# An attention and token-mixing kernel: the scale of u from a bound on u in place of its measured maximum, with the work order searched anew

## The chip, the cores and the metric

The kernel runs on one NeuronCore of one Trainium2 chip. The metric is device time in microseconds (us), the median of several runs of one compiled program. A second number, the span, is the time from the first to the last instruction of one execution that was taken with the hardware profiler on; all rows below are from that execution.

Names of engines: PE multiplies matrices (PEld is its loading of stationary operands), DVE and POOL do elementwise work and reductions, ACT does activations and scaled copies, SP issues most DMA transfers. Each engine runs its instructions in the order in which the program lists them.

## The reference, cut to what matters

Inputs q, k, v have the shape [8 batches, 8 heads, 576 positions, 64]. Each batch goes through the same steps:

```python
out_d = sm_attn(mean4(q), mean4(k), mean4(v))      # attention on means over 4 positions
out_up = np.repeat(out_d, 4, axis=2)
out_local = local_attn(q, k, v)                    # |i - j| < 4
x = (out_up + out_local)                           # -> [8, 576, 512]
xt = x.transpose(0, 2, 1)
h = np.maximum(xt @ w_tok1, 0.0) @ w_tok2          # 576 -> 256 -> 576, along positions
u = x + h.transpose(0, 2, 1)
h2 = np.maximum(u @ w_ch1, 0.0) @ w_ch2            # 512 -> 1536 -> 512, along channels
return u + h2
```

## The kernel before, in words

**Numbers in two halves.** The dense products run in 16-bit floats. Each operand y is scaled by a power of two s, the 16-bit rounding of s*y is kept as its upper part, and the rest as its lower part; `mm3` (line 134) makes three products of the parts (upper-upper, upper-lower, lower-upper). ACT makes the upper parts by a scaled copy, DVE the lower parts by one `scalar_tensor_tensor`. So before u can be split, s must be known on all 128 partitions.

**How s is found for u.** In `mix`, the stream `takes` (line 736) reads u out of PSUM: for each of four channel blocks c and two chunks ch of positions (256 and 320) ACT copies the block to `u` (line 755), and DVE takes the largest absolute value of each row into a column of `umx` (line 757). When all blocks are there, `scale_of` calls `everywhere` (line 669): DVE reduces the columns to one (line 673, tile `um_m`), PE transposes it (line 676, `um_t`), DVE reduces the row (line 679), PE spreads the value to all partitions by a product with ones (line 682, `um_b`), and `pow2` (lines 140 to 142) makes the scale `us` and its inverse `ui`. I call these steps the chain.

**The batches.** Batch 0 takes the plain way: `scaled` finds a scale for each chunk (two chains) and splits u into `uh` (lines 781 and 783), `first` makes the 512 to 1536 product tile by tile (12 tiles of 128 rows, with matmuls written "c<-uh,CW" in the trace), and `second` the 1536 to 512 product. Batches 1 to 7 use seven block products in place of eight (Strassen's scheme in Winograd's form) for the first channel product, and batches 2 to 7 for the second too. For this, `mixtures` forms sums of quarter blocks of u on POOL (line 804, eight instructions of 288 columns a batch: s1, s2, s4, s3), `upper` casts the seven operands on ACT (line 820, 14 instructions a batch), `lower` makes the lower parts on DVE (line 831, 14 a batch), and `product7` multiplies ("P<-a11h,CW" is the first of the seven). One chain a batch serves them all.

**Weights.** The inputs w_ch1 and w_ch2 arrive as 64-bit values and are converted on the chip (`to_f32`: ACT line 241, POOL lines 244 and 247, DVE line 252), then scaled and split (`parts`, lines 374 and 376): tile CW is the first channel weight, CX the second. The sums of weight blocks that the seven products need are written to DRAM once and read back in each batch through SP (tiles `t`, `w_a`, `w_s`, in six buffers of tag `ts`).

**What sets the order.** Every part of the program is a Python generator (a stream) that yields one step at a time: an engine, an estimated duration, what it needs, and which PSUM banks it takes or gives. `drive` (line 182) picks among the streams' next steps the one that could start first by a planner's clocks; among those of one engine that could start within 0.15 us of it, the one whose name stands first in the list `ORDER` (line 36) is taken. The list names about 330 streams (e3.7 is the eighth channel stream of batch 3, n5.2 the third stream of mix of batch 5, b4.6 an attention stream). Until both chunks of batch 0 are split, `drive` also puts filler products (`keep_busy`, line 175) on PE where it would idle. The order that comes out is fixed at compile time, for all engines and for the DMA issues of SP.

**Where the change acts.** `BUFS` (line 72), `value_scale` (line 320, makes `up`, `down` and `big` from the largest sum of squares of v, chain `vm`), `First.scale` (line 389), `everywhere` (669), `takes` (736), `scale_of` (761), `scaled` (769), `upper` (809), and `ORDER` with `SWITCH` (what the planner adds when PE changes the kind of its work).

Of the kernel before, what the change touches and what calls it, by code (L numbers as in the profile page):

```python
# [6 lines left out]
F32 = mybir.dt.float32  # L7
# [7 lines left out]
ALU = mybir.AluOpType  # L15
AX = mybir.AxisListType
# [17 lines left out]
SWITCH = 0.1  # L34
SHARED = 1.4
ORDER = ("e7.9 n3.2 e3.11 b3.3 b3.1 b5.0 n6.2 A6 b4.6 n4.3 e5.6 e6.11 W1 b5.6 n5.3 b3.2 e7.2 b7.9 W0 m4 n7.4 "
# [11 lines left out]
         "e3.7 e3.13 b2.5 b4.4 b4.5 e4.12 e1.7 h2 e3.2 C2 C5 e2.5 n4.5 e2.4 e4.3 C6 n7.5 b6.4 b5.3 ").split()  # L48
# [7 lines left out]
def tile_ups_attention_mixer(ctx, tc, qk, vw, vr, w1, w2, c1, c2, out):  # L56
# [15 lines left out]
    BUFS = dict(cw=6, h=6, vm=2, bs=2, bs2=4, w=4, xh=2, x=5, u=6, uh=7, ts=6, qk=4, qd=1, vw=2, vd=1, pt=2, od=1, sm=10, ev=4, nm=4, qs=1, sc=20)  # L72
# [247 lines left out]
    def value_scale(st):  # L320
# [6 lines left out]
        e = yield step("V", 0.8, give="g")  # L327
        root(big, 2.0 ** 20, st.big[:, 0:1], st.big[:, 1:2])
        nc.vector.tensor_mul(st.up, whole[:, 0:1], st.big[:, 1:2])
        nc.vector.tensor_mul(st.down, whole[:, 1:2], st.big[:, 0:1])  # L330
        make(("scale", b), e)
# [48 lines left out]
    class First(Channel):  # L380
# [8 lines left out]
        def scale(self):  # L389
            for q in range(NQ):  # L390
# [4 lines left out]
                root(big, 2.0 ** (4.5 + 0.5 - 8), self.inv[q], self.s[q])  # L395
# [273 lines left out]
    def everywhere(name, cols, n=128):  # L669

        m = T([n, 1], F32, "ev", f"{name}_m")
        yield step("V", 0.08)
        nc.vector.tensor_reduce(m, cols, axis=AX.X, op=ALU.max)
# [11 lines left out]
    def mix(st):  # L685
# [50 lines left out]
        def takes():  # L736
            for f in range(2):
# [7 lines left out]
                st.hid.append(ht)  # L745
            make(("hid", b), e)
            st.umx = T([128, 2, 4], F32, "sc", f"umx{b}")
            st.u = {}
            for ch, two in WALK[b > 0]:
                s0, N = CHUNKS[ch]  # L750
                for c in (2 * two, 2 * two + 1):
                    yield step("A", 0.06 + N * 0.00113, ("t2", b, ch, c), give=f"gg>{b}" if c % 2 else "")
                    if ch == 0:
                        st.u[c] = T([128, S], F32, "u", f"u{b}_{c}")
                    nc.scalar.activation(st.u[c][:, s0:s0 + N], banks[ch, c // 2][:, c % 2, :N], AF.Copy, scale=st.down)  # L755
                    e = yield step("V", 0.05 + N * 0.00112)
                    nc.vector.tensor_reduce(st.umx[:, ch, c:c + 1], st.u[c][:, s0:s0 + N], axis=AX.X, op=ALU.max,  # L757
                                            apply_absolute_value=True)
                    make(("u", b, ch, c), e)

        def scale_of(ch, cols):
            big = yield from everywhere(f"um{b}_{ch}", cols)
            inv = st.ui[ch] = T([128, 1], F32, "sc", f"ui{b}_{ch}")
            s = T([128, 1], F32, "sc", f"us{b}_{ch}")
            yield step("V", 0.45, give="g")
            pow2(big, 2.0 ** -5, inv, s)
            return s
# [636 lines left out]
```

## Time and profile before

| | us |
|---|---|
| median of 3 runs | 914.3 (912.48 to 918.25) |
| the profiled execution, its own time | 922.99 |
| its span | 921.2 |
| PE busy | 860.3 (93%) |
| DVE busy | 681.7 (74%) |
| ACT busy | 496.0 (54%) |
| POOL busy | 395.1 (43%) |
| granted PE clock, mean over the span | 0.963 of 2.4 GHz |

How to read it: the profiled execution is one run with the profiler on, and its own time, 922.99 us, is its span and 1.8 us around it; it is 8.7 us (1.0%) above the median of the timed runs. A busy PE is not a PE at its peak, since matmuls are pipelined. Idle time of an engine that nobody waits for costs nothing.

### The profile page before, as it was taken

Reading aid. Unit: us, or ns where it says so; the run is one execution under the profiler, and the core shown is the slowest. Engines: PE = TensorE matmul, PEld = TensorE weight load, DVE = VectorE, ACT = ScalarE, POOL = GpSimd, SP = SyncE. Lnnn points to the kernel's source line nnn. Section 1 sums busy time; section 2 is a strip of 40 time slices with the busy share of each in tenths; the row PEclk is TensorE's granted clock in tenths of the full one; section 3 lists DMA queues with packets and bytes.
Section 4 is the critical chain, followed back from the end, with each engine's and each line's share of the span. In section 5 each row is a group of like instructions: output and inputs, shape, how many; then the busy total and the mean of one; then the engine's idle time right before and its main releaser. Section 6 shows DMA issues by size and latency. Waiting matters only on the chain.

```text
span 921.2 us, 27379 instructions
## 1 busy us (share of the span) xinstructions
PE 860.3 (93%) x10961; PEld 640.2 (69%) x10969; DVE 681.7 (74%) x1564; ACT 496.0 (54%) x1208; POOL 395.1 (43%) x585
## 2 busy tenths in 40 slices
PE   6867799999998899989999899999999999999997
PEld 3534587867775777778776677678776767777775
DVE  7677879885877587884797759685899627955962
ACT  4545675435653347672577536764587435734640
POOL 4686784387424783740215521362247120212220
PEclk8756899999999999999999999999999999999999
DMA  8735333172336635725516544734555243245245
GB/s 255 218 126 195 109 133 83 48 239 80 87 85 180 163 108 174 161 64 170 148 54 204 161 120 127 202 115 140 150 167 153 68 123 113 69 140 159 80 130 164
DMA packets 101583, 125.85 MB, mean 137 GB/s; under 512 B 20016, under 2 KB 87344, under 8 KB 100208
## 3 DMA queue, kind: packets, MB, share of 16 engines
q1 hardware_dynamic: 100816, 123.51, 45.9%
q8 instruction: 86, 1.41, 0.7%
q10 hardware_dynamic: 640, 0.59, 0.2%
q14 instruction: 41, 0.34, 0.1%
HBM read 104.40 MB, written 17.30 MB: 132 GB/s over the span
## 4 chain that ended last, share of the span: by engine, by line
PE 59%; DVE 25%; ACT 5%; DMA 4%; issue 4%; POOL 1%; SPq 1%; DVEq 0%; ACTq 0%; POOLq 0%
PE P L136 17%; PE t L136 8%; PE R L136 8%; PE c L136 6%; PE Q L136 4%; PE av L660 3%; PE ad L590 2%; PE t L726 2%; PE busy L180 2%; DVE h L1015 1%; PE pT L647 1%; PE sd L562 1%; PE td L581 1%; PE sc L624 1%; DVE P L636 1%
## 5 line engine op out<-in xcount | busy, mean ns | idle before, releaser
L136 PEld LDWEIGHTS <-CW 128*128 128x128 f16 x1296 | 124.1, 98 | 43.0 <-issue 10.7
L1049 POOL TENSOR_TENSOR g<-r,g 128x288 f16<-128x288 f32 x36 | 29.7, 825 | 169.6 <-ACT g L1038 162.5
L136 PEld LDWEIGHTS <-w_s 128*128 128x128 f16 x864 | 83.1, 98 | 23.2 <-DMA w_s<-sums_s 1.6
L136 PEld LDWEIGHTS <-t 128*128 128x128 f16 x756 | 73.3, 98 | 20.2 <-issue 0.6
L136 PEld LDWEIGHTS <-w_a 128*128 128x128 f16 x648 | 62.5, 99 | 23.7 <-DMA w_a<-sums_a 5.0
L510 POOL TENSOR_TENSOR vr<-vr 72x256 f32<-72x256 f32 x64 | 49.0, 766 | 66.9 <-ACT dump L506 66.5
L136 PE MATMUL c<-h,CX 128*128 128x256 f16 (+1 forms) x576 | 76.6, 287 | 0.0
L136 PEld LDWEIGHTS <-CX 128*128 128x128 f16 x576 | 55.3, 98 | 15.1 <-issue 1.2
L755 ACT ACTIVATE u<-t,down 128x256 f32<-128x256 f32 (+1 forms) x64 | 30.2, 498 | 64.4 <-PE t L136 64.2
L136 PE MATMUL P<-h,w_a 128*128 128x288 f16 x432 | 59.3, 291 | 5.0 <-DMA w_a<-sums_a 3.4
L136 PE MATMUL t<-xh,W 128*128 128x512 f16 (+1 forms) x240 | 59.9, 390 | 2.6 <-DVE xh L704 2.6
L757 DVE TENSOR_REDUCE umx<-u 128x1 f32<-128x256 f32 (+1 forms) x64 | 27.9, 448 | 44.3 <-ACT u L755 44.2
L136 PE MATMUL P<-g,w_s 128*128 128x288 f16 x432 | 58.2, 286 | 0.9 <-DMA w_s<-sums_s 0.9
L536 POOL TENSOR_TENSOR qs<-qk 128x288 f32<-128x288 f32 x56 | 43.9, 785 | 30.1 <-DMA qk<-in_qk_dram 27.2
L136 PE MATMUL t<-W,hid 128*128 128x256 f16 (+1 forms) x384 | 54.8, 291 | 1.0 <-ACT u L755 1.0
L804 POOL TENSOR_TENSOR s<-u,u 128x288 f32<-128x288 f32 x14 | 10.8, 797 | 103.0 <-ACT u L755 103.0
L574 ACT ACTIVATE pd<-sd,nmd 72x144 f32<-72x144 f32 x128 | 37.6, 373 | 28.6 <-DVE nmd L569 26.6
L506 ACT ACTIVATE dump<-vr 72x512 uint8<-72x512 f32 x64 | 40.3, 630 | 18.9 <-DMA vr<-in_vr_dram 18.7
L590 PE MATMUL ad<-vd,ptd 72*72 72x65 f32 x512 | 40.6, 234 | 6.0 <-POOL vd L511 2.0
L704 DVE SCALAR_TENSOR_TENSOR xh<-x,back,xh 128x512 f16<-128x512 f32 (+1 forms) x40 | 33.6, 839 | 15.6 <-ACT xh L702 15.6
L590 PEld LDWEIGHTS ad<-vd,ptd 72*72 72x72 f32 x512 | 38.7, 150 | 9.2 <-POOL vd L511 4.2
L665 ACT ACTIVATE x<-av,up 128x512 f32<-128x512 f32 (+1 forms) x40 | 27.3, 688 | 32.6 <-PE av L660 32.6
(224 smaller groups left out, 2190.5 us busy)
## 6 DMA issues: line engine op xcount, KB each, us to landing
qk<-in_qk_dram SPq DMA_DIRECT2D x32, 579.0 KB
w_s<-sums_s SPq DMA_DIRECT2D x144, 128.0 KB
t<-sums SPq DMA_DIRECT2D x126, 128.0 KB
w_a<-sums_a SPq DMA_DIRECT2D x108, 128.0 KB
vw<-in_vw_dram SPq DMA_DIRECT2D x32, 351.0 KB
vr<-in_vr_dram SPq DMA_DIRECT2D x64, 144.0 KB
C_raw<-in_c_dram SPq DMA_DIRECT2D x16, 512.0 KB
out_dram<-u SPq DMA_DIRECT2D x48, 144.0 KB
```

Source lines behind the costliest of these rows:

```text
L136: nc.tensor.matmul(ps, lhs(a), rhs(c), start=first and i == 0, stop=last and i == 2, **kw)
L506: nc.scalar.activation(dump, t.rearrange("p r c -> p (r c)"), AF.Square, scale=2.0 ** -20, accum_out=st.vm[:, i:i + 1])
L510: nc.gpsimd.tensor_add(t[:, 0:2], t[:, 0:2], t[:, 2:4])
L536: nc.gpsimd.tensor_add(two, x[:, :, 0:2], x[:, :, 2:4])
L574: nc.scalar.activation(pd[:, par, g], s[:, par, g], AF.Exp, bias=nm[:, par, g:g + 1], scale=0.125 / 16)
L590: nc.tensor.matmul(ps[:, g, par], pt[:, par, kg, G * g:G * g + G], st.vd[:, kg, 2 * pr + par], start=kg == 0, stop=kg == 1)
L660: nc.tensor.matmul(ps[QB * j:QB * j + QB, par, D * hp:D * hp + D], pt[p, hp, QB * j:QB * j + QB], st.vw[h][p, g, D * hp:D * hp + D], start ...
L665: nc.scalar.activation(x.rearrange("p hp two d -> p two hp d"), ps[:n, :, :4 * D].rearrange("p two (hp d) -> p two hp d", hp=4), AF.Copy, ...
L704: nc.vector.scalar_tensor_tensor(st.xh[t][:, 1], xf(t), back[:n], st.xh[t][:, 0], ALU.mult, ALU.subtract)
L755: nc.scalar.activation(st.u[c][:, s0:s0 + N], banks[ch, c // 2][:, c % 2, :N], AF.Copy, scale=st.down)
L757: nc.vector.tensor_reduce(st.umx[:, ch, c:c + 1], st.u[c][:, s0:s0 + N], axis=AX.X, op=ALU.max, apply_absolute_value=True)
L1049: e_.tensor_tensor(o[:, 1], plain[p, FROM[x]], o[:, 0], ALU.subtract)
```

## The change

It removes the eight row maxima of u in each batch (64 DVE instructions) and the chain behind them. In their place the largest upper half of `hid` (the hidden values of the token product, known before u) is taken by one DVE reduction over 1024 elements of 16 bits a batch, spread by the same chain, and put into a bound: most = 516 * down * max(hid) + 4 * big, with `down` and `big` from `value_scale`, by one more small DVE instruction. The scale comes from that bound. Batch 0 uses one scale for both chunks (one chain in place of two) and casts each block of u as soon as that block is there. Two small DVE instructions are added in `value_scale`, 8 times. The constants in `pow2` and in `First.scale` change by factors of 4. The buffers of two tags of small tiles change, `SWITCH` goes from 0.1 to 0.05, and the list `ORDER` is another.

```diff
--- before.py
+++ after.py
@@ -31,21 +31,21 @@
 
 SLACK = 0.4
 HOP = 0.2
-SWITCH = 0.1
+SWITCH = 0.05
 SHARED = 1.4
-ORDER = ("e7.9 n3.2 e3.11 b3.3 b3.1 b5.0 n6.2 A6 b4.6 n4.3 e5.6 e6.11 W1 b5.6 n5.3 b3.2 e7.2 b7.9 W0 m4 n7.4 "
 ...
-         "e3.7 e3.13 b2.5 b4.4 b4.5 e4.12 e1.7 h2 e3.2 C2 C5 e2.5 n4.5 e2.4 e4.3 C6 n7.5 b6.4 b5.3 ").split()
+ORDER = ("e3.11 e6.8 e7.13 e1.3 e5.4 e3.9 b3.5 W1 n7.2 e7.8 e5.11 e6.11 b5.7 b3.0 e7.1 U0 a7 e6.1 H0 b2.4 m4 "
 ...
+         "P1 P0 b4.4 e5.13 A1 b7.5 n2.0 M1 e6.5 e6.2 e6.13 e7.0 b7.3 e7.7 e6.7 e1.7 n5.3 b5.6 b5.4 ").split()
 PX = 7
 PATH = [(c, ch) for ch in range(2) for c in range(4)], [(c, ch) for c in range(4) for ch in range(2)]
 WALK = ((0, 0), (0, 1), (1, 0), (1, 1)), ((0, 0), (1, 0), (0, 1), (1, 1))
@@ -69,7 +69,7 @@
     sb = ctx.enter_context(tc.tile_pool(name="sb", bufs=1))
     dram = ctx.enter_context(tc.tile_pool(name="dram", bufs=1, space=bass.MemoryType.DRAM))
     psum = ctx.enter_context(tc.tile_pool(name="psum", bufs=1, space=bass.MemoryType.PSUM))
-    BUFS = dict(cw=6, h=6, vm=2, bs=2, bs2=4, w=4, xh=2, x=5, u=6, uh=7, ts=6, qk=4, qd=1, vw=2, vd=1, pt=2, od=1, sm=10, ev=4, nm=4, qs=1, sc=20)
+    BUFS = dict(cw=6, h=6, vm=2, bs=2, bs2=6, w=4, xh=2, x=5, u=6, uh=7, ts=6, qk=4, qd=1, vw=2, vd=1, pt=2, od=1, sm=10, ev=4, nm=4, qs=1, sc=16)
 
     SLOTS = dict(gg=2, m=3, g=1, w=4, t=9)
     now_in = {k: 0 for k in SLOTS}
@@ -324,10 +324,13 @@
         big = yield from everywhere(f"vm{b}", st.vm, G)
         st.big = T([128, 2], F32, "bs", f"big{b}")
         st.up, st.down = (T([128, 1], F32, "bs2", f"{x}{b}") for x in ("up", "down"))
-        e = yield step("V", 0.8, give="g")
+        e = yield step("V", 1.0, give="g")
         root(big, 2.0 ** 20, st.big[:, 0:1], st.big[:, 1:2])
         nc.vector.tensor_mul(st.up, whole[:, 0:1], st.big[:, 1:2])
         nc.vector.tensor_mul(st.down, whole[:, 1:2], st.big[:, 0:1])
+        st.most = T([128, 2], F32, "bs2", f"most{b}")
+        nc.vector.tensor_scalar(st.most[:, 0:1], st.big[:, 0:1], 4.0, None, ALU.mult)
+        nc.vector.tensor_scalar(st.most[:, 1:2], st.down, 516.0, None, ALU.mult)
         make(("scale", b), e)
 
     def u32(ap):
@@ -392,7 +395,7 @@
                 big = yield from everywhere(f"C1_n{q}", self.mx[:, q:q + 1])
                 e = yield step("V", 0.45, give="g")
 
-                root(big, 2.0 ** (4.5 + 0.5 - 8), self.inv[q], self.s[q])
+                root(big, 2.0 ** (4.5 + 0.5 - 6), self.inv[q], self.s[q])
                 make(("C1", "scale", q), e)
                 for i in range(4 * q, 4 * q + 4):
                     yield from self.parts(i)
@@ -666,11 +669,11 @@
                              ps[:n, :, :4 * D].rearrange("p two (hp d) -> p two hp d", hp=4), AF.Copy, scale=st.up[:n])
         make(("x", b, t), e)
 
-    def everywhere(name, cols, n=128):
+    def everywhere(name, cols, n=128, us=0.08, *needs):
 
         m = T([n, 1], F32, "ev", f"{name}_m")
-        yield step("V", 0.08)
-        nc.vector.tensor_reduce(m, cols, axis=AX.X, op=ALU.max)
+        yield step("V", us, *needs)
+        nc.vector.tensor_reduce(m, cols, axis=AX.X if len(cols.shape) == 2 else AX.XY, op=ALU.max)
         yield step("F", 0.11, take="g")
         ps = P1(f"{name}_t")
         nc.tensor.transpose(ps[0:1, :n], m, ident[:n, :n])
@@ -743,37 +746,38 @@
                 e = yield step("V", 0.61, give=f"gg>{b}" if f else "")
                 nc.vector.scalar_tensor_tensor(ht[:, 1], st.acc[:, f], 0.0, ht[:, 0], ALU.max, ALU.subtract)
                 st.hid.append(ht)
+            st.tops = both[:, :, 0]
             make(("hid", b), e)
-            st.umx = T([128, 2, 4], F32, "sc", f"umx{b}")
             st.u = {}
             for ch, two in WALK[b > 0]:
                 s0, N = CHUNKS[ch]
                 for c in (2 * two, 2 * two + 1):
-                    yield step("A", 0.06 + N * 0.00113, ("t2", b, ch, c), give=f"gg>{b}" if c % 2 else "")
+                    e = yield step("A", 0.06 + N * 0.00113, ("t2", b, ch, c), give=f"gg>{b}" if c % 2 else "")
                     if ch == 0:
                         st.u[c] = T([128, S], F32, "u", f"u{b}_{c}")
                     nc.scalar.activation(st.u[c][:, s0:s0 + N], banks[ch, c // 2][:, c % 2, :N], AF.Copy, scale=st.down)
-                    e = yield step("V", 0.05 + N * 0.00112)
-                    nc.vector.tensor_reduce(st.umx[:, ch, c:c + 1], st.u[c][:, s0:s0 + N], axis=AX.X, op=ALU.max,
-                                            apply_absolute_value=True)
                     make(("u", b, ch, c), e)
 
-        def scale_of(ch, cols):
-            big = yield from everywhere(f"um{b}_{ch}", cols)
-            inv = st.ui[ch] = T([128, 1], F32, "sc", f"ui{b}_{ch}")
-            s = T([128, 1], F32, "sc", f"us{b}_{ch}")
-            yield step("V", 0.45, give="g")
-            pow2(big, 2.0 ** -5, inv, s)
+        def scale_of():
+
+            yield step("V", 0.0, ("hid", b))
+            big = yield from everywhere(f"um{b}", st.tops, 128, 1.1)
+            inv = st.ui[0] = st.ui[1] = T([128, 1], F32, "sc", f"ui{b}")
+            s = T([128, 1], F32, "sc", f"us{b}")
+            most = T([128, 1], F32, "sc", f"mu{b}")
+            yield step("V", 0.55, give="g")
+            nc.vector.tensor_scalar(most, big, st.most[:, 1:2], st.most[:, 0:1], ALU.mult, ALU.add)
+            pow2(most, 2.0 ** -7, inv, s)
             return s
 
         def scaled():
             for ch in range(2):
                 s0, N = CHUNKS[ch]
-                yield step("V", 0.0, *(("u", b, ch, c) for c in range(4)))
-                s = yield from scale_of(ch, st.umx[:, ch])
+                if ch == 0:
+                    s = yield from scale_of()
                 uh = st.uh[ch] = []
                 for c in range(4):
-                    yield step("A", 0.06 + N * 0.00113, *([("C1", NF - 1)] if (ch, c) == (1, 3) else []))
+                    yield step("A", 0.06 + N * 0.00113, ("u", b, ch, c), *([("C1", NF - 1)] if (ch, c) == (1, 3) else []))
                     if ch == 1 or c % 2 == 0:
                         t = T([128, 2 - ch, 2, N], F16, "uh", f"uh{b}_{ch}_{c}")
                     o = t[:, c % (2 - ch)]
@@ -808,9 +812,8 @@
 
         def upper():
 
+            st.us = yield from scale_of()
             yield step("V", 0.0, *all_u)
-            st.us = yield from scale_of(0, st.umx.rearrange("p a c -> p (a c)"))
-            st.ui[1] = st.ui[0]
             for name in ORDER7:
                 for i in range(2):
                     e = yield step("A", 0.42, *([("h", b - 1)] if b > 1 else [("h", 0, ch, NF - 1) for ch in range(2)] + [("C2", NF - 1)]),
```

## Rows read from the trace of the kernel before

**Rows 1.** The page: busy time of each engine, and granted PE clock in 40 slices.
```profile
PE 860.3 (93%) x10961; PEld 640.2 (69%) x10969; DVE 681.7 (74%) x1564; ACT 496.0 (54%) x1208; POOL 395.1 (43%) x585
...
PEclk8756899999999999999999999999999999999999
```

**Rows 2.** Windows, three stretches: PE, PEld, DVE, ACT, POOL busy us (instructions), clock, DMA, GB/s.
```profile
92.30:116.60 24.30, 19.32 (x132) 13.02 (x133) 21.82 (x49) 15.18 (x28) 18.98 (x17) 0.85 0.39 128
116.60:162.30 45.70, 44.84 (x627) 35.40 (x626) 40.46 (x100) 29.08 (x71) 29.43 (x46) 1.00 0.32 96
...
235.20:921.20 686.00, 658.01 (x8326) 499.46 (x8323) 497.81 (x1156) 371.29 (x934) 239.06 (x360) 0.99 0.46 132
```

**Rows 3.** DVE groups by shape, removed reductions: busy us, mean ns | idle before, releaser.
```profile
L757 DVE TENSOR_REDUCE umx<-u 128x1 f32<-128x320 f32 x32 | 14.9, 481 | 20.2 <-ACT u L755 20.1
...
L757 DVE TENSOR_REDUCE umx<-u 128x1 f32<-128x256 f32 x32 | 13.0, 416 | 24.1 <-ACT u L755 24.0
```

**Rows 4.** DVE groups by shape: the nearest rows to what is added.
```profile
L550 DVE TENSOR_REDUCE qd<-qk 128x144 f32<-128x576 f32 x4 | 3.0, 742 | 0.0
...
L141 DVE TENSOR_SCALAR ui<-ui 128x1 f32<-128x1 f32 x9 | 1.4, 153 | 0.3
```

**Rows 5.** Timeline, batch 0: start us, duration us, instruction.
```profile
94.30 0.69 DVE L744 SCALAR_TENSOR_TENSOR hid<-t,hid 128x512 f16<-128x512 f32 x1
...
101.41 0.46 ACT L755 ACTIVATE u<-t,down 128x256 f32<-128x256 f32 x1
...
106.25 0.14 DVE L673 TENSOR_REDUCE um_m<-umx 128x1 f32<-128x4 f32 x1
...
109.33 0.16 DVE L142 RECIPROCAL us<-ui 128x1 f32<-128x1 f32 x1
...
114.97 0.48 DVE L783 SCALAR_TENSOR_TENSOR uh<-u,us,uh 128x256 f16<-128x256 f32 x1
...
116.63 1.61 PE L136 MATMUL c<-uh,CW 128*128 128x256 f16 x12
```

**Rows 6.** Windows within the stretch of rows 5, columns as in rows 2.
```profile
100.00:105.00 5.00, 4.83 (x33) 3.34 (x33) 4.84 (x8) 3.60 (x8) 4.68 (x5) 1.00 0.00 0
105.00:110.00 5.00, 2.84 (x16) 1.38 (x15) 4.93 (x14) 2.51 (x6) 3.69 (x4) 1.00 0.74 224
110.00:116.60 6.60, 4.74 (x32) 2.68 (x33) 6.50 (x17) 3.76 (x8) 5.91 (x6) 0.76 0.87 300
```

**Rows 7.** Tile CX: duration ns min/median/max, first and last start us.
```profile
L136 PE MATMUL c<-h,CX x576: 270/298/421, 158.4 to 355.9; 128*128 128x256 f16 x96, 128*128 128x320 f16 x96
...
L374 ACT ACTIVATE CX<-CX,C_s x12: 721/722/722, 145.6 to 168.8; 128x512 f16<-128x512 f32 x12
```

**Rows 8.** Timeline, batch 2: start us, duration us, instruction, idle before.
```profile
438.02 0.95 ACT L755 ACTIVATE u<-t,down 128x320 f32<-128x320 f32 x2 [1.89 <-PE t L136]
...
443.23 0.16 DVE L142 RECIPROCAL us<-ui 128x1 f32<-128x1 f32 x1
...
451.53 0.90 PE L136 MATMUL P<-a11h,CW 128*128 128x288 f16 x6
...
453.91 0.94 DVE L831 SCALAR_TENSOR_TENSOR a22h<-u,us,a22h 128x288 f16<-128x288 f32 x2
```

**Rows 9.** Window around the stretch of rows 8, columns as in rows 2.
```profile
436.00:456.00 20.00, 19.76 (x223) 15.59 (x223) 14.40 (x36) 9.15 (x22) 6.57 (x8) 1.00 0.51 148
```

**Rows 10.** Lines 804 and 831, batches 1 to 7: columns as in rows 7.
```profile
L804 POOL TENSOR_TENSOR s<-u x14: 792/1004/1035, 233.9 to 846.7; 128x288 f32<-128x288 f32 x14
...
L831 DVE SCALAR_TENSOR_TENSOR a11h<-u,us,a11h x14: 505/518/1054, 233.5 to 844.3; 128x288 f16<-128x288 f32 x14
```

**Rows 11.** PE's waits: us in total, times, longest us.
```profile
PE P L136 <- DVE m L979: 3.5, 6, 1.4
PE P L136 <- DMA w_a<-sums_a: 3.4, 2, 2.2
```

**Rows 12.** Window just after one such wait for a transfer, columns as in rows 2.
```profile
740.00:745.00 5.00, 4.00 (x19) 2.59 (x20) 0.00 (x0) 0.40 (x1) 0.00 (x0) 0.66 0.61 178
```

22 rows, old and new, of the table ORDER are left out of this document.

## The prediction, made before the change was run

> **What bounds the kernel now.** I read the page's busy shares and its clock line first, then busy time by windows, the chain of waits, the timeline at the two places where the removed steps stand, and PE's waits. PE is busy for 860.3 of 921.2 us and DVE for 681.7, and the clock line shows full speed (9) from its seventh slice on, below that before [rows 1]. The windows say where PE's remaining time lies: from 235.2 us to the end it is busy for 658.0 of 686.0 us while DVE has 497.8, so what is left to win there is 28.0 us at most, and DVE is not the limit; from 116.6 to 162.3 it is busy for 44.84 of 45.70 [rows 2]. Before 116.6 it is otherwise: in the 24.3 us up to that point PE runs at 0.85 of its clock, a part of it on filler products that feed nothing, and DVE is busy for 21.82 of 24.3 [rows 2]. So the kernel has a start, in which DVE and the arrival of weights set the pace, and a long dense part, set by PE. A change that takes work from DVE and shortens a wait for DVE can be worth something in the start, and little in the dense part.
>
> **The change part by part.** All sums are against the profiled execution's own 923.0 us; it stands 8.7 us above the median of 914.3, and I carry the difference over unchanged.
>
> *The removed and added DVE work.* 32 reductions of 320 elements and 32 of 256 go: 14.9 + 13.0 = 27.9 us, or 4 x 0.481 + 4 x 0.416 = 3.59 us a batch [rows 3]. No row shows a reduction over 1024 elements of 16 bits. From the two shapes one more element costs (481 - 416) / 64 = 1.02 ns, and the row of 576 elements, 742 ns, leaves 155 ns fixed [rows 3, 4]; 1024 elements make 155 + 1044 = 1.20 us. Its lower end is two elements at a time, 155 + 522 = 0.68 us; its upper end 2.5 us, if it were slowed beside POOL as lower parts are at worst, 1054 against 505 ns [rows 10]. I take 1.20, from the rows of the same operation. The Trainium skill ("VectorE: DVE Perf Modes", The perf-mode tier table) says that a reduction works on one element at a time even for 16-bit data, which speaks against the lower end; the 32-bit rows agree with their 1.02 ns, and no row here shows 16 bits. Three small instructions (one for the bound, two in value_scale) add 3 x 0.153 = 0.46 us [rows 4]. So DVE loses 3.59 - 1.20 - 0.46 = 1.93 us a batch, 15.4 in 8 (at the ends 5 and 20), plus about 0.6 for the second chain of batch 0: 16 of 682 us. In the dense part this pays only where PE waits for DVE. The largest such wait is 3.5 us in six pieces [rows 11]; I count 1 us, between 0 and 3.5. Cover: PE's own work.
>
> *The start.* The hidden values of batch 0 are ready at 94.30 + 0.69 = 95.0 us, the last u of the first chunk at 101.41 + 0.46 = 101.9. But the chain's first reduction runs only at 106.25, behind weight conversions and the second chunk's maxima in DVE's order, the scale is there at 109.5, the last lower part at 114.97 + 0.48 = 115.45, and PE's first channel product begins at 116.63 [rows 5]: 14.7 us after u. With the bound, the reduction can run at 95.0, and the chain from its first reduction takes 109.5 - 106.25 = 3.25 us, so the scale could stand at 95.0 + 1.2 + 3.25 + 0.15 = 99.6, before u itself. Then a cast and a lower part behind the last u (0.48 us is the row of the last lower part, and I take 0.5 for each) and the same 1.2 us to PE give 101.9 + 0.5 + 0.5 + 1.2 = 104.1: at most 12.5 us earlier. That is the upper end. The lower end comes from DVE: between 100 and 116.6 us it is busy for 4.84 + 4.93 + 6.50 = 16.27 of 16.6 us [rows 6], so pulling four lower parts forward pushes weight conversions back. They are needed too: the casts of the second weight, CX, run from 145.6 us, and the first product with it at 158.4 [rows 7]. If these stay where they are, PE finishes its first products sooner and then waits, and the gain is 0. DVE work actually saved in this stretch is 3.59 + 0.6 - 1.2 - 0.15 = 2.8 us, and DVE idles for 45.70 - 40.46 = 5.2 us between 116.6 and 162.3 [rows 2], into which pushed-back conversions can go: 2.8 + 5.2 = 8.0. Between 0 and 12.5, with 2.8 assured by the saved work and 8.0 by what DVE can absorb, I take 5.5 us. What is late next is the chain of conversions, norms and casts of CX.
>
> *The joints of the dense part.* In batches 1 to 7 the chain stands between u and the seven products. In batch 2 u ends at 438.02 + 0.95 = 438.97 and the scale at 443.39: 4.4 us, and the last lower part ends at 454.85 [rows 8]. But PE is busy for 19.76 of the 20 us around it [rows 9]: the remaining block products of the batch before lie over the chain. So the 4.4 us of waiting, seven times, are covered today; the 0.24 us that PE idles at a joint are all that can be had directly, 7 x 0.24 = 1.7 us. What appears in the chain's place is the POOL work of line 804, which still must follow u, eight instructions of 0.8 to 1.0 us. With the scale there before u, the 14 lower parts start beside those eight instead of after most of them. Where they meet now, DVE goes from 505 to 1054 ns at worst, and the last pair on POOL has a median of 1004 against a least of 792 [rows 10]. The Trainium skill ("SBUF — State Buffer", Who interferes with whom) has the mechanism: a DVE instruction with two inputs in SBUF and a GpSimd one that reads SBUF exclude each other; the slow rows agree. Eight meetings of 1054 - 505 = 0.55 us make 4.4 us, as much as the chain gave. I count the joints at 1.5 us for all seven, between -2 and +4, because PE's other work hides them either way.
>
> *The moved work.* The new ORDER moves nearly every step: PE's groups, DVE's and ACT's steps, and the DMAs that SP issues in its order (products' weights, q and v of the next batch, and outputs). Their count stays the same. PE's work is the same but for three small matmuls of one chain, so only waits change. Those that end on a transfer now, such as 3.4 us in two pieces [rows 11], may shrink, grow or move. I see no row that gives the sign, so 0, with 6 us either way (twice those 3.4 us, about a fifth of PE's 28.0 us of idle time). SWITCH acts only in the planner, the buffers and constants change no duration.
>
> Sum: 1 + 5.5 + 1.5 + 0 = 8 us. 923.0 - 8 = 915.0 in profile terms, 914.3 - 8 = **906 us** (0.9% faster).
>
> **The rivals.**
>
> *A. The start gives nearly all it can.* Ten of the 12.5 us come through because conversions of CX are put into idle DVE time, the joints give their 4 and the DVE waits 2: 16 us, 898. For it: the 14.7 us between u and the first product, most of it queueing [rows 5], and a search that can now put these steps anywhere. Against: DVE is full in just that stretch [rows 6].
>
> *B. Nothing arrives.* The chain is hidden at every joint [rows 9], and in the start CX keeps its time: PE begins earlier and waits before 158.4 [rows 7]. Only 1 to 2 us remain: 913. For it: PE is at 96 to 98% in all stretches behind 116.6 [rows 2]. This is also the case in which the change does what it says and its object wasn't on the path.
>
> *C. Slower, by transfers that come late.* The block weights come through six buffers on SP's one queue, in ORDER's sequence. If the new order puts a load of q, or an issue that waits for a buffer, in front of them, PE waits as it did for w_a, 2.2 us at the longest [rows 11], and the clock then drops: the granted clock is 0.66 of full speed in the five microseconds behind one such wait, a mix of its two levels of 1.2 and 2.4 GHz [rows 12], worth another 5 x 0.34 = 1.7 us. So 3.9 us each. One more in each of the six batches with such loads costs 23.4 us against the 8 won: 929. It decides from the fifth on: 5 x 3.9 - 8 = 11.5 us, over 1%. For it: such waits exist with the present order, and a planner's clocks are no trace. Against: only two pieces of them are in the largest group now.
>
> **How the numbers follow.** My forecast has 0.42, A 0.22, B 0.20, C 0.16. The runs shown lie within 0.6%, so about 1%, 9 us, is what a measurement can tell from no change. Faster by over 1% (below 905.2) is A and nearly half of the forecast's own spread: 0.22 + 0.20 = 0.42. Within 1%: the rest of the forecast, 0.22, most of B, 0.19, and a mild C, 0.03: 0.44. Slower: 0.14. The range goes from 893 (A with some 5 us of luck in the order) to 922 (B with 6 us of bad luck and a little more); the forecast's own is 899 to 912.
>
> **What would show it.** Right: line 757 gone, a new reduction near 1.2 us, eight times; DVE's busy time near 666 us; the first "c<-uh,CW" near 111 instead of 116.6; PE still at about 96% behind it. The scale of batch 2 before its u, and its lower parts slower beside POOL. Wrong: an unchanged start of the first product with CX although the first channel product came forward (B), PE's waits on w_a, w_s or t longer than 10 us in all or further slices of lower clock (C), or a first product before 107 us with everything behind it moved as far (A).

## The result, and the profile after

The changed kernel takes 905.4 us (median of 9 runs, 901.85 to 913.07); the kernel before, on the same chips, 919.35 us (9 runs, 912.48 to 925.79). The ratio is 0.986, with a 95% interval of 0.982 to 0.990: 1.4% faster, some 13 us, where 906 us and 0.9% had been forecast. The two profiled executions stand further apart than the medians, 921.2 us of span before and 902.4 after, because that of before was 3.6 us above its median and that of after 0.9 us below. So differences between the two traces read some 5 us too large in all.

The page of the changed kernel, busy shares and clock:

```profile
PE 853.4 (95%) x10970; PEld 636.4 (71%) x10977; DVE 686.1 (76%) x1519; ACT 495.7 (55%) x1208; POOL 404.6 (45%) x585
...
PEclk9878899999999989999999999999999999999999
```

DVE lost 64 reductions and is nevertheless busy for 4.4 us more than before [rows 1]. The windows, cut at the same events as before: PE's first channel product of batch 0, the first product with CX, and the first seven-block product of batch 1 (columns as in rows 2).

```profile
92.30:101.60 9.30, 8.67 (x69) 6.25 (x69) 9.20 (x14) 5.80 (x12) 7.53 (x7) 1.00 0.22 68
101.60:139.00 37.40, 35.09 (x512) 27.88 (x512) 33.47 (x72) 25.56 (x61) 27.39 (x39) 0.95 0.42 143
139.00:224.60 85.60, 84.15 (x1284) 63.99 (x1280) 73.10 (x170) 39.30 (x91) 51.84 (x89) 1.00 0.42 121
224.60:902.40 677.80, 655.87 (x8190) 498.44 (x8188) 499.59 (x1116) 373.29 (x936) 253.39 (x365) 0.99 0.47 135
```

The first product begins at 101.6 us where it was 116.6, and the first seven-block product of batch 1 at 224.6 where it was 235.2 [rows 2]: 10.6 of the 18.8 us of span lie before that. The dense stretch behind it takes 677.8 in place of 686.0 us, and PE idles in it for 677.8 - 655.9 = 21.9 in place of 28.0 us.

The timeline of batch 0, the same steps as in rows 5:

```profile
89.28 0.69 DVE L747 SCALAR_TENSOR_TENSOR hid<-t,hid 128x512 f16<-128x512 f32 x1
...
90.94 1.20 DVE L676 TENSOR_REDUCE um_m<-hid 128x1 f32<-128x1024 f16 x1
...
92.06 1.41 DVE L379 SCALAR_TENSOR_TENSOR CW<-CW,C_s,CW 128x512 f16<-128x512 f32 x1
...
95.49 1.56 DVE L252 SCALAR_TENSOR_TENSOR CX<-C_raws 128x512 uint32<-128x512 uint32 x1
...
95.66 0.47 ACT L758 ACTIVATE u<-t,down 128x256 f32<-128x256 f32 x1 [0.51 <-PE t L136]
...
97.64 0.17 DVE L142 RECIPROCAL us<-ui 128x1 f32<-128x1 f32 x1
...
101.60 1.13 PE L136 MATMUL c<-uh,CW 128*128 128x256 f16 x7
...
103.77 1.28 DVE L787 SCALAR_TENSOR_TENSOR uh<-u,us,uh 128x256 f16<-128x256 f32 x1
...
105.10 0.38 PE L136 MATMUL c<-uh,CW 128*128 128x256 f16 x2 [1.38 <-DVE uh L787]
```

The new reduction is there. The scale is ready at 97.8 us, 1.7 us behind the last u of the first chunk, where it came 7.6 us behind it before. PE starts with the operands that it has and waits for the fourth lower part. From the end of the hidden values to PE's first product it is 101.60 - 89.97 = 11.6 us, before 116.63 - 95.0 = 21.6 [rows 5].

That the hidden values themselves came 5.0 us sooner can't be the bound's gain: of the change only two DVE instructions of 0.15 us and the other order run before them. It is in the main the execution that was profiled. From 60 to 80 us the granted clock of the kernel before was 0.50, the lower of its two levels; the kernel with the bound and the old list (first experiment below), whose PE instructions up to the hidden values are the same in the same order, fillers apart, ran there at 0.97 and had its hidden values at 87.7 us. The kernel before, then that one:

```profile
60.00:80.00 20.00, 16.29 (x312) 11.13 (x314) 11.04 (x24) 8.76 (x15) 10.09 (x9) 0.50 0.73 257
```

```profile
60.00:80.00 20.00, 14.49 (x358) 9.23 (x358) 17.28 (x30) 14.00 (x24) 15.93 (x14) 0.97 0.89 333
```

So times are best counted from the end of batch 0's hidden values (the second `hid` instruction on DVE). Then batch 1's first seven-block product comes after 134.6 us, before after 140.2, and the end after 812.4, before after 826.2: 5.6 us in the start and 8.2 in the dense part, together 13.8, about as far as the medians are apart.

In batch 2 the casts now follow u at once, and the lower parts meet POOL's sums of quarter blocks:

```profile
433.50 0.95 ACT L758 ACTIVATE u<-t,down 128x320 f32<-128x320 f32 x2 [1.89 <-PE t L136]
...
434.62 0.55 ACT L823 ACTIVATE a11h<-u,us 128x288 f16<-128x288 f32 x1
...
435.62 1.99 POOL L808 TENSOR_TENSOR s<-s,u 128x288 f32<-128x288 f32 x2
...
436.87 2.02 DVE L834 SCALAR_TENSOR_TENSOR s1h<-s,us,s1h 128x288 f16<-128x288 f32 x2
```

The first cast comes 0.2 us behind u, where the scale alone came 4.4 us behind it [rows 8]. But two lower parts of s1 take 2.02 us, and two sums on POOL 1.99. Grouped by shape (busy us, mean ns | idle before), the kernel before had

```profile
L831 DVE SCALAR_TENSOR_TENSOR a11h<-u,us,a11h 128x288 f16<-128x288 f32 x14 | 9.2, 695 | 1.8 <-ACT a11h L820 1.8
L831 DVE SCALAR_TENSOR_TENSOR s1h<-s,us,s1h 128x288 f16<-128x288 f32 x14 | 7.8, 581 | 0.0
...
L831 DVE SCALAR_TENSOR_TENSOR a22h<-u,us,a22h 128x288 f16<-128x288 f32 x14 | 6.7, 509 | 1.0 <-ACT a22h L820 1.0
```

and the changed one

```profile
L834 DVE SCALAR_TENSOR_TENSOR a11h<-u,us,a11h 128x288 f16<-128x288 f32 x14 | 12.5, 928 | 30.2 <-ACT a11h L823 30.2
L834 DVE SCALAR_TENSOR_TENSOR s1h<-s,us,s1h 128x288 f16<-128x288 f32 x14 | 12.0, 892 | 0.0
...
L834 DVE SCALAR_TENSOR_TENSOR a22h<-u,us,a22h 128x288 f16<-128x288 f32 x14 | 6.7, 510 | 0.1
```

The operands that are split while POOL works take longer, a11 by a third and s1 by a half; the last, a22, does not. Over all seven operands the lower parts take 64.2 us, before 53.5.

### The profile page after: what moved, and what is told of

Read it like the earlier page. It is cut to its first block, busy times and chain, and to the rows that moved or that the text cites. A ratio compares the mean times of both kernels' runs of the same rounds, so it can differ in the third digit from the quotient of the medians.

```text
span 902.4 us, 27311 instructions
## 1 busy us (share of the span) xinstructions
PE 853.4 (95%) x10970; PEld 636.4 (71%) x10977; DVE 686.1 (76%) x1519; ACT 495.7 (55%) x1208; POOL 404.6 (45%) x585
## 4 chain that ended last, share of the span: by engine, by line
PE 59%; DVE 24%; DMA 7%; ACT 4%; issue 3%; POOL 2%; SPq 1%; ACTq 0%; DVEq 0%; POOLq 0%
PE P L136 18%; PE t L136 9%; PE R L136 8%; PE c L136 7%; PE Q L136 4%; PE av L663 3%; PE ad L593 2%; PE t L729 2%; DMA W_raw<-in_w_dram 2%; PE pT L650 2%; DMA C_raw<-in_c_dram 1%; PE sd L565 1%; DMA vw<-in_vw_dram 1%; DVE h L1018 1%; DVE P L639 1%
## 5 line engine op out<-in xcount | busy, mean ns | idle before, releaser
L136 PEld LDWEIGHTS <-w_s 128*128 128x128 f16 x864 | 82.9, 98 | 24.1 <-DMA w_s<-sums_s 2.6
L136 PEld LDWEIGHTS <-t 128*128 128x128 f16 x756 | 73.5, 98 | 19.8 <-issue 0.4
L513 POOL TENSOR_TENSOR vr<-vr 72x256 f32<-72x256 f32 x64 | 53.0, 829 | 61.6 <-ACT dump L509 61.3
L136 PEld LDWEIGHTS <-w_a 128*128 128x128 f16 x648 | 62.2, 98 | 21.6 <-issue 3.2
L509 ACT ACTIVATE dump<-vr 72x512 uint8<-72x512 f32 x64 | 40.1, 627 | 13.5 <-DMA vr<-in_vr_dram 13.4
L641 ACT ACTIVATE P<-P 128x304 f32<-128x304 f32 (+1 forms) x40 | 18.3, 457 | 50.2 <-DVE P L639 49.9
L136 PEld LDWEIGHTS <-hid 128*128 128x128 f16 x384 | 37.3, 100 | 10.8 <-issue 1.0
L1052 POOL TENSOR_TENSOR g<-u,g 128x288 f16<-128x288 f32 x36 | 30.2, 839 | 31.2 <-ACT g L1041 31.2
```

The source lines that it names most:

```text
L136: nc.tensor.matmul(ps, lhs(a), rhs(c), start=first and i == 0, stop=last and i == 2, **kw)
L509: nc.scalar.activation(dump, t.rearrange("p r c -> p (r c)"), AF.Square, scale=2.0 ** -20, accum_out=st.vm[:, i:i + 1])
L513: nc.gpsimd.tensor_add(t[:, 0:2], t[:, 0:2], t[:, 2:4])
L641: nc.scalar.activation(w, w, AF.Exp, scale=0.125)
L1052: e_.tensor_tensor(o[:, 1], plain[p, FROM[x]], o[:, 0], ALU.subtract)
```

## The experiments

Two questions: is the gain the bound's or the list's, and if it is the bound's, does it come in batch 0 or at the joints of batches 1 to 7? Every kernel was compared with the kernel before on the same chip.

**The bound alone, with the old list.** Edit, with the old list in place of the new one:

```diff
-SWITCH = 0.05
+SWITCH = 0.1
```

> The changed kernel with the list ORDER and the SWITCH of the kernel before, so the bound alone. Theory S (the start): the bound shortens the way from u to the first channel product of batch 0 and the rest is carried over; ratio to the kernel before 0.985 to 0.993, first 'c<-uh,CW' at 107 us or earlier against 116.6. Rival O (the order): the gain is that of the new list; with the old one the ratio is 0.997 to 1.015, even if the first product comes earlier.

Measured: 927.35 us, ratio 1.0159 (1.0122 to 1.0195): slower than the kernel before, just above rival O's range. The end of the hidden values, then tile uh and tile a11h (duration, first and last start):

```profile
87.02 0.69 DVE L747 SCALAR_TENSOR_TENSOR hid<-t,hid 128x512 f16<-128x512 f32 x1
...
L136 PE MATMUL c<-uh,CW x288: 269/290/310, 99.6 to 151.9; 128*128 128x256 f16 x72, 128*128 128x320 f16 x72
...
L136 PE MATMUL P<-a11h,CW x252: 282/286/448, 222.1 to 883.3; 128*128 128x288 f16 x126
```

Each theory is half right. The start gains without any new list: first product at 99.6 in place of 116.6, first seven-block product of batch 1 at 222.1 in place of 235.2. Of these 17.0 and 13.1 us, 7.3 lie before the hidden values. Counted from there the first product comes after 11.9 in place of 21.6 us, and batch 1's first seven-block product after 134.4 in place of 140.2, 5.8 us sooner. Behind that, 926.1 - 222.1 = 704.0 us in place of 686.0: the old list loses 18 us in the dense part on the changed work.

**The new list alone, on the kernel before.** Edit: ORDER and SWITCH of the change, and nothing else.

> The kernel before with the new ORDER and SWITCH, so the order alone. Theory S: no gain without the bound, ratio 0.998 to 1.015, first channel product of batch 0 no earlier than 112 us. Rival O: ratio 0.985 to 0.993.

Measured: 951.19 us, ratio 1.0414 (1.0366 to 1.0462). Neither list is any good on the other version. The size is beyond what theory S named, and its 112 us for the first product were missed too.

```profile
86.86 0.69 DVE L744 SCALAR_TENSOR_TENSOR hid<-t,hid 128x512 f16<-128x512 f32 x1
...
L136 PE MATMUL c<-uh,CW x288: 269/290/310, 107.3 to 162.7; 128*128 128x256 f16 x72, 128*128 128x320 f16 x72
...
L136 PE MATMUL P<-a11h,CW x252: 282/286/444, 243.2 to 906.6; 128*128 128x288 f16 x126
```

From 243.2 to the end of its span, 949.3, it is 706.1 us. The first product comes 9.3 us sooner than in the kernel before, but 7.4 of them lie before the hidden values; from there it is 19.8 us, near the 21.6 of the old list.

**Batch 0 undone.** Edit, the maximum in place of the bound for one batch:

```diff
-                if ch == 0:
+                if b == 0:
+                    yield step("V", 0.0, *(("u", b, ch, c) for c in range(4)))
+                    s = yield from scale_of(ch, st.umx[:, ch])
+                elif ch == 0:
                     s = yield from scale_of()
```

> The changed kernel with the new order, but batch 0 measures the largest u again (8 reductions and two chains); batches 1 to 7 keep the bound. Theory S: most of the gain goes, ratio 0.995 to 1.003, first channel product at 110 us or later. Rival J (the joints: what counts is the earlier scale in batches 1 to 7 and the DVE work saved there): the gain stays, ratio 0.985 to 0.991.

Measured: 917.15 us, ratio 1.0044 (1.0019 to 1.0068). The whole gain is gone, just above theory S's 0.995 to 1.003; rival J's 0.985 to 0.991 was missed, and so were theory S's 110 us for the first product.

```profile
86.71 0.69 DVE L750 SCALAR_TENSOR_TENSOR hid<-t,hid 128x512 f16<-128x512 f32 x1
...
L136 PE MATMUL c<-uh,CW x288: 269/290/310, 107.4 to 162.2; 128*128 128x256 f16 x72, 128*128 128x320 f16 x72
...
L136 PE MATMUL P<-a11h,CW x252: 283/286/445, 236.2 to 871.9; 128*128 128x288 f16 x126
```

Its dense part takes 914.3 - 236.2 = 678.1 us, as long as the changed kernel's 677.8. So the difference is the start alone: 236.2 - 224.6 = 11.6 us at batch 1's first product, 11.9 us at the end. But that is not the price of the maximum. Counted from the hidden values, batch 1's first product comes after 148.8 us, 14.2 later than in the changed kernel and 8.6 later than in the kernel before, which measures the maximum too, under its own list. So some 8.6 of the 14.2 us are this list's loss on work that it was not searched for. The run shows that the dense part keeps its 678 us when batch 0 alone is undone; that the whole gain comes from batch 0 it does not show, and rival J is not refuted by it.

**Batches 1 to 7 undone.** Edit: the same branch for `b > 0`, in `takes` and `upper`.

> The changed kernel with the new order, but batches 1 to 7 measure the largest u again (56 reductions, chain behind u); batch 0 keeps the bound. Theory S: the gain stays but for some 2 us, ratio 0.985 to 0.991. Rival J: ratio 0.995 to 1.003.

Measured: 946.39 us, ratio 1.0381 (1.0324 to 1.0439), far outside both. PE's first product keeps its gain (at 103.6 us, 11.6 behind the hidden values), but the dense part takes 951.1 - 232.4 = 718.7 us, longer than in either original. This can't be the price of seven chains and 56 reductions alone, with which the kernel before needs 686.0; another plan made from the same list is the likely cause. So this run does not separate the theories.

**What a list is worth.** Two random draws of ORDER, each for both versions, with SWITCH at 0.05.

```diff
-ORDER = ("e3.11 e6.8 e7.13 ...
+ORDER = <the same names, shuffled>
```

> The kernel before, with ORDER shuffled at random (first draw) and SWITCH 0.05: a list fitted to neither version. If a searched list is worth 20 to 30 us of the dense part (as the two mismatched runs suggest), the ratio to the kernel before is 1.03 to 1.07. If a list matters little and only mismatch hurts, it is 1.00 to 1.02.

> The changed kernel with the same shuffled list as s1_max. Theory S: the bound gains in the start whatever the list, so 8 to 16 us less than s1_max, with the first seven-block product of batch 1 (P<-a11h) earlier by as much. Rival O: no gain outside a search, within 5 us of s1_max.

> As s1_max with a second random draw; the difference between s1_max and s2_max is the scatter that a list brings, expected 5 to 15 us.

> As s1_bound with the second draw: theory S 8 to 16 us less than s2_max, rival O within 5 us of it.

Measured: first draw 1051.26 us without and 1051.02 with the bound (ratios 1.1461 and 1.1445), second draw 1034.35 and 1006.01 (1.1279 and 1.0981). A searched list of these 285 names (not some 330, as stated above) is worth 100 to 145 us here, many times the bound and far more than the 1.03 to 1.07 expected; the two draws without the bound lie 17 us apart, where 5 to 15 were expected. Hidden values and batch 1's first product, second draw, without and with the bound:

```profile
99.11 0.69 DVE L732 SCALAR_TENSOR_TENSOR hid<-t,hid 128x512 f16<-128x512 f32 x1
...
L124 PE MATMUL P<-a11h,CW x252: 282/286/448, 295.2 to 987.5; 128*128 128x288 f16 x126
```

```profile
99.93 0.68 DVE L735 SCALAR_TENSOR_TENSOR hid<-t,hid 128x512 f16<-128x512 f32 x1
...
L124 PE MATMUL P<-a11h,CW x252: 283/286/447, 278.0 to 960.7; 128*128 128x288 f16 x126
```

That is 17.2 us sooner; in the first draw it was 269.4 against 266.1, 3.3 us. In the end 28 us and nothing. Theory S's 8 to 16 us was met by neither pair, rival O's 5 us by the first alone. Under four lists there are now kernels without and with the bound. In us from the end of batch 0's hidden values, one trace each, without -> with:

| list | PE's first product of batch 0 | first seven-block product of batch 1 | end |
|---|---|---|---|
| old | 21.6 -> 11.9 | 140.2 -> 134.4 | 826.2 -> 838.4 |
| new | 19.8 -> 11.6 | 155.6 -> 134.6 | 861.8 -> 812.4 |
| first draw | 18.9 -> 10.9 | 171.1 -> 168.4 | 950.5 -> 953.8 |
| second draw | 20.7 -> 13.5 | 195.4 -> 177.4 | 930.3 -> 902.0 |

So the bound brings PE's first product forward by 7 to 10 us under every list tried. What is left of it at batch 1 ranges from 2.7 to 21 us, and at the end it is anything from a loss of 12 us, under the list searched for the other version, to a gain of 49, under the list searched for this one.

**The same work, another planner constant.**

```diff
-SWITCH = 0.05
+SWITCH = 0.1
```

on the changed kernel, with the new list.

> The changed kernel with SWITCH at 0.1 as before the change, and the new ORDER: not one piece of work differs, only what the planner adds when PE changes its kind of work. If a list is worth its gain only for the very plan on which it was searched, the time grows by 1 to 4% as in the mismatched runs: ratio 0.997 to 1.03. If the mismatched runs were slow because of the work they changed, it stays within 0.5%: 0.983 to 0.990.

Measured: 952.76 us, ratio 1.0417 (1.0372 to 1.0461), beyond the first theory's upper end: 5.6% above the changed kernel with not one piece of work changed. The window from batch 1's first product, at 219.5 us, to the end:

```profile
219.50:951.20 731.70, 671.83 (x8213) 505.64 (x8211) 505.32 (x1121) 372.08 (x937) 251.40 (x366) 0.97 0.43 125
```

PE idles there for 59.9 us, against 21.9 in the changed kernel, and is busy for 671.8 in place of 655.9 at a granted clock of 0.97; ACT and POOL have the same work as before to within 2 us. A list is a key to one plan: here one figure of the planner made another plan, and what the search had won was lost. That is enough to account for the mismatched runs, though it was not shown for each.

Three more kernels therefore add work without the planner's knowing, so that all other instructions keep their order.

**The reductions put back, unread.**

```diff
                     nc.scalar.activation(st.u[c][:, s0:s0 + N], banks[ch, c // 2][:, c % 2, :N], AF.Copy, scale=st.down)
+                    nc.vector.tensor_reduce(unused[:, 4 * ch + c:4 * ch + c + 1], st.u[c][:, s0:s0 + N], axis=AX.X, op=ALU.max,
+                                            apply_absolute_value=True)
```

> The changed kernel, every other instruction in the same order, with the 64 reductions over u put back on DVE right behind the casts; nothing reads them and the planner doesn't know of them. If DVE's time has cover (the step 'this pays only where PE waits for DVE'), 27.9 us of work cost 0 to 6 us: ratio to the kernel before 0.986 to 0.993. If DVE sets the pace, 15 us and more: 1.002 or above.

Measured: 912.49 us, ratio 0.9961 (0.9929 to 0.9993). By the ratios that is 1.0% of 916 us, some 9 us, more than in the changed kernel; against the last run below (PE's start held back), which holds a small delay of its own and took 905.98 us on the same chip, it is 6.5 us. So 27.9 us of work cost 6.5 to 9 us: between the two. Tile unused:

```profile
L761 DVE TENSOR_REDUCE unused<-u x64: 400/445/489, 90.3 to 832.7; 128x1 f32<-128x256 f32 x32, 128x1 f32<-128x320 f32 x32
its engine sat idle before it (us, times) until:
  ACT u L760: 45.6, 32
```

The reductions are short, but 32 of them hold DVE's queue until ACT has cast u, 45.6 us in all. In the kernel before they wait as well [rows 3], but there the planner had placed them. The dense part grew from 677.8 to 686.6 us.

**The scale late by seven hand-overs.** In batches 1 to 7 the scale passes seven times from DVE to ACT and back before the casts.

```diff
+            x = st.u[3][:, S - 1:S]
+            for k in range(7):
+                nc.vector.tensor_scalar(pause[:, 2 * k:2 * k + 1], x, 1.0, None, ALU.mult)
+                nc.scalar.activation(pause[:, 2 * k + 1:2 * k + 2], pause[:, 2 * k:2 * k + 1], AF.Copy, scale=1.0)
+                x = pause[:, 2 * k + 1:2 * k + 2]
+            nc.vector.scalar_tensor_tensor(us, x, 0.0, st.us, ALU.mult, ALU.add)
```

> The changed kernel, same order, but in batches 1 to 7 the scale passes seven times from DVE to ACT and back once the last u is there, some 4 us as the measured chain took, and only then do the casts start. If the joints are covered by PE's other work (as predicted), 0 to 3 us in all: 0.986 to 0.990. If the earlier scale is what the new order lives on, up to 7 x 4 = 28 us: 1.00 to 1.02.

Measured: 918.21 us, ratio 1.0034 (1.0007 to 1.0062): 16 us by the ratios, 12 against that last run on the same chip; in the upper range. The dense part takes 916.1 - 222.2 = 693.9 us. In batch 2:

```profile
437.48 0.94 ACT L761 ACTIVATE u<-t,down 128x320 f32<-128x320 f32 x2 [1.89 <-PE t L136]
...
441.28 0.38 ACT L1120 COPY m<-R 128x288 f32<-128x288 f32 x1
441.41 0.49 DVE L826 SCALAR_TENSOR_TENSOR late<-pause,us 128x1 f32<-128x1 f32 x1 [0.27 <-ACT pause L823]
441.93 0.53 ACT L834 ACTIVATE a11h<-u,late 128x288 f16<-128x288 f32 x1 [0.27 <-DVE late L826]
```

The first cast comes 441.93 - 438.42 = 3.5 us behind u, 3.3 more than in the changed kernel; seven times that is 23 us put in, and 12 to 16 came out. So at the new list's joints such a delay is not covered, where in the kernel before PE was busy for 19.76 of 20 us around the chain [rows 9]. Two things keep this from showing that the new list lives on the early scale. The hand-overs hold ACT's and DVE's queues too: the copy `m<-R` starts at 441.28, 2.9 us behind the last u, where in the changed kernel it started at 434.34, right behind the casts of u. And the same delay was not put into the kernel before. The groups of lower parts show the meeting with POOL from the other side, since in batch 2 they start when three of its four pairs of sums are done:

```profile
L845 DVE SCALAR_TENSOR_TENSOR a11h<-u,late,a11h 128x288 f16<-128x288 f32 x14 | 7.8, 595 | 3.7 <-ACT a11h L834 3.7
...
L845 DVE SCALAR_TENSOR_TENSOR s1h<-s,late,s1h 128x288 f16<-128x288 f32 x14 | 6.7, 512 | 0.4 <-ACT s1h L834 0.4
```

595 and 512 ns against 928 and 892 in the changed kernel, for the same instructions.

**PE's start held back.** The fourth operand of batch 0's first chunk goes through a copy by DMA.

```diff
+                    if ch == 0 and c == 3:
+                        nc.scalar.dma_start(copied, o)
+                        o = copied
                     uh.append(o)
```

> The changed kernel, same order, but the first channel product of batch 0 reads one of its four operands through a copy by DMA, so PE starts it some 2 to 3 us later while DVE, ACT and POOL go on. If the start is on the path (theory S), all of it passes to the end: 2 to 3 us, ratio 0.988 to 0.990. If what follows waits for CX's conversions anyway (the rival 'Nothing arrives'), 0 to 1 us: 0.986 to 0.987.

Measured: 905.98 us, ratio 0.9904 (0.9876 to 0.9932). PE waited 3.5 us for the copy, where it had waited 1.4 us for the operand, 2.1 us more; the ratio is 0.4% higher, 4 us, but the intervals overlap (0.982 to 0.990 for the change) and its profiled span was even shorter, 900.4 us. The first products of the kernels that share this order up to there lie at 97.5 to 101.6 us, so executions scatter by more than the delay put in. Nearly all of that scatter lies before the hidden values; from there to PE's first product it is 11.6 to 11.9 us in all of them. Counted so, 0.9 of the 2.1 us are left at batch 1's first product (135.5 against 134.6) and 0.7 at the end (813.1 against 812.4), one trace each. That leans to the second theory, but with the ratios it is not decided.

## Why the prediction was right, and where it was not

**Direction, size and reason.** Forecast were 8 us, 5.5 in the start and 2.5 in the dense part; measured are 13. Counted from the hidden values the two traces differ by 13.8 us, 5.6 in the start and 8.2 in the dense part. So the start came out at its forecast size at batch 1's first product, and under the old list it is 5.8 us; what was mis-sized, by a factor of three, is the dense part: the saved DVE work (1 us), the joints (1.5) and the moved order (0) together. That the forecast of 906 us lies so near the measured 905.4 is luck in part: it set out from 914.3, the median of three runs, and nine runs of the same kernel gave 919.35. The 8.7 us by which the profiled execution stood above that median, which I carried along unexplained, lie to a good part before the hidden values: 94.99 us against 87.7 with the same list, at a granted clock of 0.50 against 0.97. (The clock line reaches 9 from its sixth slice on, not its seventh.) How far the dense part of the kernel before scatters no run shows, since there is one trace of it; two traces with the changed kernel's order gave 677.8 and 677.6 us.

*The start*, 5.5 us between 0 and 12.5. At PE's first product 10.0 of the 12.5 us came (21.6 to 11.6 behind the hidden values), which is rival A's size; at batch 1's first product 5.6 are left. So the sum came out at the end of the stretch, but its bounds, 2.8 us of saved DVE work and 8.0 us of room on DVE, did not bind at PE's first product: it came 10 us sooner although DVE was full in the 16.6 us before it [rows 6], which said only that DVE had its instructions in that order. And what I named as late next, the first product with CX, came forward with the rest under the new list, from 63.4 to 49.0 us behind the hidden values (158.4 to 139.0 us [rows 7]), since the casts of CX start at 126.4 in place of 145.6; under the old list it stayed (61.7 us), and batch 1's first product came forward all the same. What uses up the other 4 us before batch 1 I have not traced. That the scale would stand before u was wrong: from its first reduction the chain took 97.8 - 90.9 = 6.9 us in place of 1.2 + 3.25 + 0.15, since weight conversions stand between its DVE steps.

*The DVE work.* The reduction was forecast at 1.20 us and is 1.20, on the side of the Trainium skill's rule ("VectorE: DVE Perf Modes", The perf-mode tier table) that 16-bit data make a reduction no faster. DVE's busy time was forecast at 666 us and is 686: the step that failed was to take the saved 16 us as they stood, after pricing the meetings with POOL at up to 4.4 us a batch in another term. The lower parts took 10.7 us more. Of the rest, 7.7 us lie in three groups of DVE instructions on halves of 288 columns (`g<-x,g` 21.5 to 25.5 us, `m<-m,r` 17.7 to 19.7, `h<-m,h` 21.0 to 22.7); what they meet I have not traced. The Trainium skill's rule that such a DVE instruction and a GpSimd one reading SBUF exclude each other ("SBUF — State Buffer", Who interferes with whom) agrees with the rows: 892 ns beside POOL and 512 after it for the same instruction. That DVE's saved time would pay only 1 us, at most 3.5, was likely too little: put back at the fixed new order, which has no place for them, the reductions cost 6.5 to 9 us. I had looked at what waits for them (almost nothing) and not at what stands behind them in DVE's queue while they wait for ACT, though rows 3 have it: 20.2 + 24.1 us of idle time before them.

*The joints*, 1.5 us. No run speaks against the chain having been covered in the kernel before. But the cover was the old list's choice: at the fixed new order a scale 3.3 us late, with ACT's and DVE's queues held, costs 12 to 16 us. Either of the two, the reductions or the late scale, is as large as the 8.2 us that the dense part gained, so the bound can account for all of it; how much of it is the bound's and how much the new search's stays open.

*The moved work*, 0 with 6 us either way, was the worst of the sizes. A plan that is not fitted to the work costs 22 to 47 us against the same version under its own list: the same work with one planner constant changed is 5.6% slower, the old list on the changed work 1.6% slower than before. The sum came out only because both lists had been fitted to their own version. Rival C's mechanism, late transfers, did not come: PE's waits for w_a and w_s fell from 4.3 to 2.2 us. Rival B (nothing arrives) fell with the 5.6 us that are left at batch 1.

## What to carry to other kernels

Where the order of all work is compiled in from a searched list, price a change with each version under its own searched list; one list for both measures the mismatch, here 1.6% slower with the old list and 5% faster with the new one, where it is 1.4%. Before you read a gain off two traces, count from the last event that the change can't have touched: here 5.0 of the 18.8 us lay ahead of it. A scale that can be bounded ahead of its data shortened the start under every list tried; how much of that reached the end depended on the list. And an instruction that waits in an engine's queue can cost what stands behind it, even when nobody reads its result: 27.9 us of unread reductions cost 6.5 to 9 us here.

## What the runs showed of the hardware

A reduction of 1024 16-bit elements took 1200 to 1210 ns in all eight batches, on the line through the 32-bit rows of 256, 320 and 576 elements (1.02 ns an element and 155 ns). The small DVE instruction that takes two scalars per partition out of SBUF and its data out of PSUM (`mu`, one element wide) took 270 ns, where the one with constants that read such a tile out of PSUM in the kernel before (`ui<-um_b`) took 157. And with the 64 unread reductions put back, 27.9 us of work, DVE's busy time rose by only 705.8 - 686.1 = 19.7 us. Some 3.6 us of the difference are rows of neighbouring DVE instructions that overlap at their ends, which the busy time counts once; the other 4.6 are shorter durations in other groups. Fewer meetings of the lower parts with POOL are not the reason as far as a11 and s1 go: they took 928 and 893 ns, as in the changed kernel.
